# Seven half-size products in place of eight in block A's x^T phi(k), with its operand sums on VectorE

## The chip, the cores and the metric

The kernel runs on one core of a Trainium2 chip. Its time is the device time of one launch in microseconds; the kernel before takes 199.45 us (median of three runs, 199.34 to 199.52).

## The reference

Two blocks of linear attention, A and B, share the input x (2048 x 640) and have weights of their own; a gate computed from x mixes their outputs. There are 32 heads of 20 columns. Products take bfloat16 operands.

```python
qkv = (x @ wqkv)                                   # q, k, v, each 2048 x 640
phi = lambda t: jnp.where(t > 0, t + 1, jnp.exp(t)) + 1e-6
pq, pk = phi(q), phi(k)
kv  = jnp.einsum("bhsd,bhse->bhde", pk, v)         # per head 20 x 20
z   = jnp.einsum("bhsd->bhd", pk)
num = jnp.einsum("bhqd,bhde->bhqe", pq, kv)
den = jnp.einsum("bhqd,bhd->bhq", pq, z)[..., None] + 1e-6
block = (num / den) @ wo
g = sigmoid((x * gate_w).sum(-1, keepdims=True))
out = g * a + (1 - g) * b                          # a, b: the two blocks
```

## The kernel before

v is never formed. Since v = x wv, the sum over the rows of phi(k)^T v is taken as wv^T (x^T phi(k)): the kernel computes G = x^T phi(k), a 640 x 640 matrix whose inner dimension is the 2048 rows, then `kvt_pass` multiplies it with wv and masks it to the heads (KVT), and `m_unit` multiplies KVT with wo into M. The output is a product of the normalised phi(q) with M for both blocks, itself computed from quarter blocks with operand sums (class `Pair`, L431 to L477).

On the chip the 2048 rows are 16 chunks of 128 (ST), the 640 columns are five blocks of 128 (DT) or two halves of 320 (HF). `xn` holds x with rows on the partitions, `xT` its transpose, `pk` holds phi(k) by rows, `pqT` holds phi(q) transposed, `GT` holds G by row blocks of 128.

PSUM is used as four slots of two banks (`ps`, L63). A slot is handed out in turn or by number, and a new use waits until the last reader of the old one is done.

The stages of block A, in the order in which TensorE runs them:

- `k_chunk` (L195), 16 times: ten matmuls of 320 columns into a slot, then `phi` (L179): ScalarE takes exp out of PSUM into e; VectorE takes min(e, 1) + 1e-6 in place (L183), and then max(t + 1 + 1e-6, e), reading t out of PSUM (L184). Blocks of q for the first half of the rows (`q_block`, `q_unit`) are mixed in among them.
- `q_pass` (L492): five `q_unit`s for the second half of the rows (ten matmuls of 512 columns, `phi` on 128 x 1024); between them the gate's logits (`gate_pass`), the column sums of phi(k) (`z_rows`, zA) and their selection by head (`z_pass`, zsA).
- `g_all` (L506): five row blocks of G by `g_pass` (L246), each 16 chunks times two halves, 32 matmuls of 320 columns into one slot, evacuated by ScalarE. After the first block `rec_pass` (L338) makes the denominators (denA, 40 matmuls), which VectorE multiplies with the gate's factor and inverts (rT). Then come five `norm_unit`s (L387), two in each of the third and fourth blocks and one ahead of the fifth: eight small matmuls (exA) spread the inverses over two slots; VectorE multiplies phi(q) with the first slot directly out of PSUM, and with the second out of a bfloat16 copy (ex) that ScalarE makes.
- `p_diff` (L360): two passes of VectorE for the output's operands (D3).
- Block B's `k_chunk`s begin; `kvt_pass(0)` stands after the second of them in the program, and the `m_unit`s of A stand further on among the rest.

Block B follows with the same passes, and the output pairs close the kernel.

Up to the output stage the order on each engine is chosen by a scheduler at build time, from its own costs; only the output stage stands in a `manual_schedule`, where instructions keep the order of the program. Each engine runs its instructions in the order that it was given. Weights of the next stage are loaded by SP when the tile of the stage before has been read for the last time (wqB after q_pass).

Of the kernel before, what the change touches and what calls it, by code (L numbers as in the profile page):

```python
# [8 lines left out]
P = 128  # L9
FP32 = mybir.dt.float32  # L10
BF16 = mybir.dt.bfloat16
ACT = mybir.ActivationFunctionType
ALU = mybir.AluOpType

S, D, H = 2048, 640, 32
Dh = D // H
DT = D // P
ST = S // P
NB = 4
CB = 4  # L20
HB = 512
HF = D // 2
JW = 120
NJ = 6
EPS = 1e-6
RB = 256
SH = S // 2
# [3 lines left out]
def kernel(  # L31
# [11 lines left out]
    nc = tc.nc  # L43
# [4 lines left out]
    persist = ctx.enter_context(tc.tile_pool(name="persist", bufs=1))  # L48
    wpool = ctx.enter_context(tc.tile_pool(name="wpool", bufs=1))
    work = ctx.enter_context(tc.tile_pool(name="work", bufs=2))  # L50
# [12 lines left out]
    def ps(name, slot=None):  # L63

        return ps_raw(name, slot).bitcast(FP32).rearrange("p (b n) -> p b n", b=2)

    xT = persist.tile([P, DT, S], BF16, name="xT")
    xn = persist.tile([P, ST, D], BF16, name="xn")
    pk = persist.tile([P, ST, D], BF16, name="pk")
    pqT = [persist.tile([P, DT, S], BF16, name=f"pqT{b}") for b in "AB"]  # L70
    GT = persist.tile([P, DT, D], BF16, name="GT")
    KVT = persist.tile([P, NJ, D], BF16, name="KVT")
    M = [persist.tile([P, DT, D], BF16, name=f"M{b}") for b in "AB"]
# [6 lines left out]
    gwr = persist.tile([P, DT, H], BF16, name="gwr")  # L80
    zero = persist.tile([P, HB], BF16, name="zero")
    grow = persist.tile([1, D], BF16, name="grow")
    D3 = persist.tile([P, DT, S // 2], BF16, name="D3")
    TM = [None] * 4
    ge = [persist.tile([P, 2 * RB], FP32, name=f"ge{b}") for b in "AB"]

# [4 lines left out]
    nc.vector.memset(zero[:], 0.0)  # L91
    nc.vector.memset(ones[:], 1.0)
    nc.vector.memset(KVT[:], 0.0)
    xb0 = x2[0:CB * P, :].rearrange("(p q) d -> p q d", q=CB)
    wk = [None, None]
    wv = [None, None]
    wq = [None, None]
# [15 lines left out]
    for n in range(1, NB):  # L113
        for c in range(DT):
            nc.sync.dma_start_transpose(
                out=xT[:, c, n * HB:(n + 1) * HB], in_=x2[n * HB:(n + 1) * HB, c * P:(c + 1) * P]
# [8 lines left out]
    for sign, base in ((1, 0), (-1, Dh - 1)):  # L125
        nc.gpsimd.affine_select(
            out=maskE[:], in_=maskE[:], pattern=[[sign * P, DT], [-sign * Dh, H]],
# [3 lines left out]
    for r in range(4):  # L131
        rows = slice(32 * r, 32 * r + 32)
        for sign, base in ((1, 0), (-1, Dh - 1)):
            nc.gpsimd.affine_select(
                out=E4[rows], in_=E4[rows], pattern=[[sign, D]],
# [8 lines left out]
    def gate_columns():  # L144

        gps = ps("gps")
        for c in range(DT):
            nc.tensor.matmul(  # L148
                gps[:, 0, c * H:(c + 1) * H], lhsT=grow[0:1, c * P:(c + 1) * P], rhs=ones[0:1, :], start=True, stop=True
            )  # L150
        nc.vector.tensor_copy(out=gwr[:], in_=gps[:, 0, 0:DT * H].rearrange("p (c h) -> p c h", h=H))
# [24 lines left out]
        copy = nc.scalar.copy if eng == "act" else nc.vector.tensor_copy  # L176
        copy(out=xT[:, :, i * P:(i + 1) * P], in_=pt[:, 0:D].rearrange("p (c n) -> p c n", c=DT))

    def phi(dst, src, n):  # L179

        e = work.tile([P, 2, n], BF16, tag="e", name="e", bufs=3)
        nc.scalar.activation(out=e[:], in_=src, func=ACT.Exp)  # L182
        nc.vector.tensor_scalar(e[:], e[:], 1.0, EPS, op0=ALU.min, op1=ALU.add)  # L183
        nc.vector.scalar_tensor_tensor(out=dst, in0=src, scalar=1.0 + EPS, in1=e[:], op0=ALU.add, op1=ALU.max)  # L184

    def k_mm(b, i, c, pt, hf):
# [8 lines left out]
    def k_chunk(b, i):  # L195
        pt = ps(f"k{'AB'[b]}")
        for hf in range(2):
            for c in range(DT):
                k_mm(b, i, c, pt, hf)
        k_done(b, i, pt)  # L200
# [14 lines left out]
        for i in range(2):  # L215
            k_done(0, i, pts[i])

    def q_unit(b, m, h):

        pt = ps(f"q{'AB'[b]}")  # L220
        for u in range(2):
            for c in range(DT):
                n = 2 * h + u
                nc.tensor.matmul(  # L224
                    pt[:, u, :], lhsT=wq[b][:, c, m * P:(m + 1) * P], rhs=xT[:, c, n * HB:(n + 1) * HB],
                    start=(c == 0), stop=(c == DT - 1),
                )
        phi(pqT[b][:, m, h * 2 * HB:(h + 1) * 2 * HB].rearrange("p (b n) -> p b n", b=2), pt, HB)

    def q_block(b, m, n):  # L230

# [14 lines left out]
    def g_pass(b, c, slot, between=None):  # L246

        pt = ps(f"g{'AB'[b]}", slot)
        for i in range(ST):
            if between is not None and i == ST // 2:  # L250
                between()
            for hf in range(2):
                g_mm(c, i, hf, pt)
        evac(GT[:, c, :], pt, "act")

    def g_mm(c, i, hf, pt):
        nc.tensor.matmul(  # L257
            pt[:, hf, 0:HF], lhsT=xn[:, i, c * P:(c + 1) * P], rhs=pk[:, i, hf * HF:(hf + 1) * HF],
            start=(i == 0), stop=(i == ST - 1),
        )  # L260

    def g_last(b, c, slots):

# [74 lines left out]
    def rec_pass(b, zsel, slot):  # L338

        pt = ps(f"den{'AB'[b]}", slot)  # L340
        for h in range(2):
            by_group(pt[:, 0, h * RB:(h + 1) * RB], zsel, pqT[b], h)
        rts = []
        for h in range(2):
            part = slice(h * RB, (h + 1) * RB)
            d1 = work.tile([P, RB], FP32, tag="d1", name="d1")
            nc.vector.scalar_tensor_tensor(
                out=d1[:], in0=pt[:, 0, part], scalar=EPS, in1=ge[b][:, part], op0=ALU.add, op1=ALU.mult
            )
            rT = work.tile([P, RB], BF16, tag="rT", name="rT")  # L350
            with nc.allow_low_precision(reason="a fp32 reciprocal, stored as the bf16 that multiplies bf16"):
                nc.vector.reciprocal(out=rT[:], in_=d1[:])
            rts.append(rT)
        return rts

    def add_rows(dst, a, b, op):
        nc.vector.tensor_tensor(out=dst, in0=a, in1=b, op=op)

    def p_diff():

        for rows in (slice(0, HB), slice(HB, SH)):
            up = slice(SH + rows.start, SH + rows.stop)
            add_rows(D3[:, :, rows], pqT[0][:, :, rows], pqT[0][:, :, up], ALU.subtract)

# [24 lines left out]
    def norm_unit(b, parts, rts, slots):  # L389

        pts = [ps(f"ex{'AB'[b]}", s) for s in slots]
        for k, (m, h) in enumerate(parts):
            for j in range(4):
                nc.tensor.matmul(  # L394
                    pts[j // 2][:, j % 2, k * RB:(k + 1) * RB], lhsT=E4[32 * j:32 * j + 32, m * P:(m + 1) * P],
                    rhs=rts[h][32 * j:32 * j + 32, :], start=True, stop=True,
                )
        (m0, h0), (m1, h1) = parts
        for jj in range(2):
            src = pts[jj][:].rearrange("p j (k n) -> p j k n", n=RB)  # L400
            if h0 == h1:
                r0 = h0 * 2 * HB + jj * HB
                dst = pqT[b][:, m0:m1 + 1, r0:r0 + HB].rearrange("p k (j n) -> p j k n", n=RB)
            else:
                dst = pqT[b][:, m0, :].rearrange("p (k u j n) -> p u j k n", k=2, u=2, n=RB)[:, jj]
            if jj == 1:
                ex = work.tile([P, 2, 2, RB], BF16, tag="ex", name="ex")
                nc.scalar.copy(out=ex[:], in_=src)
                src = ex[:]
            nc.vector.tensor_tensor(out=dst, in0=src, in1=dst, op=ALU.mult)  # L410
# [68 lines left out]
    def load_w(b, which, eng):  # L479
        lo = {"q": 0, "k": D, "v": 2 * D}[which]  # L480
        t = wpool.tile([P, DT, D], BF16, tag="w" + which, name=f"w{which}{'AB'[b]}")
        eng.dma_start(out=t[:], in_=wq_dram[b][:, :, lo:lo + D])
        return t
# [8 lines left out]
    def q_pass(b, units):  # L492

        units = list(units)
        q_unit(b, *units.pop(0))
        if b == 0:
            gate_pass()
        zr = z_rows(b)
        for k in range(2):
            q_unit(b, *units.pop(0))  # L500
        zsel = z_pass(b, zr)
        for m, h in units:
            q_unit(b, m, h)
        return zsel

    def g_all(b, zsel):  # L506

        units = [((m, h), (m + 1, h)) for h in range(2) for m in (0, 2)] + [((DT - 1, 0), (DT - 1, 1))]

        def norm():  # L510
            norm_unit(b, units.pop(0), rts, (2, 3))

        g_pass(b, 0, 1)
        rts = rec_pass(b, zsel, 2)
        g_pass(b, 1, 0)
        for c in range(2, DT):
            norm()
            if b == 1 and c == DT - 1:
                g_last(b, c, (1, 0))
            else:  # L520
                g_pass(b, c, (c + 1) % 2, norm if c < DT - 1 else None)
        assert not units
# [7 lines left out]
        for m in (0, 2):  # L530
            q_block(0, m, n)
    q_unit(0, DT - 1, 0)
    for i in range(ST // 2, ST):
        if i == ST - 1:
            gate_columns()
        k_chunk(0, i)
    for n in range(1, NB):
        nc.sync.dma_start(
            out=xn[:, n * CB:(n + 1) * CB, :], in_=x2[n * HB:(n + 1) * HB, :].rearrange("(q p) d -> p q d", p=P)
        )  # L540
    wv[0] = load_w(0, "v", nc.sync)
    load_wo(0, nc.sync)
    wk[1] = load_w(1, "k", nc.sync)
    zsel = q_pass(0, [(m, 1) for m in range(DT)])
    wq[1] = load_w(1, "q", nc.sync)
    g_all(0, zsel)
    p_diff()


# [11 lines left out]
    zsel = q_pass(1, [(m, h) for h in range(2) for m in range(DT)])  # L561
    for tag, ks in (("wk", (0, 3)), ("wq", (1, 2))):
        t = wpool.tile([P, 2, DT, HF], BF16, tag=tag, name="TM" + tag)
# [12 lines left out]
    with tc.manual_schedule():  # L576
# [35 lines left out]
        for i in range(1, half):  # L612
            p, after = pairs[i], pairs[i + 1] if i + 1 < half else None
# [45 lines left out]
```

## Time and profile before

| | us |
|---|---|
| median of 3 runs | 199.45 (199.34 to 199.52) |
| the profiled execution | 200.06 |
| its span, first to last instruction | 198.3 |
| x^T phi(k) of A, from its first matmul to block B's first, by the chain of waits | 53.12 to 78.35 |
| granted TensorE clock | 1.0 of full speed throughout |

In the tables of the profile PE is TensorE's matmuls, PEld its weight loads, DVE is VectorE, ACT ScalarE, POOL GpSimd and SP the engine that issues most transfers. A line of a group gives the source line, engine and operation, what it writes and reads, shapes and types, how often, then the busy time in us and the mean of one in ns, then the idle time just before and what ended it. A window line gives, after its length, the busy time and the number of instructions of PE, PEld, DVE, ACT and POOL, then the granted clock, the share of the transfer engines' time and GB/s. A line of the list of waits gives who waited for whom, the total, how often and the longest. The chain of waits is followed back from the last instruction, at each step to what released it.

### The profile page before, as it was taken

Reading aid. Unit: us, or ns where it says so; the run is one execution under the profiler, and the core shown is the slowest. Engines: PE = TensorE matmul, PEld = TensorE weight load, DVE = VectorE, ACT = ScalarE, POOL = GpSimd, SP = SyncE. Lnnn points to the kernel's source line nnn. Section 1 sums busy time; section 2 is a strip of 40 time slices with the busy share of each in tenths; the row PEclk is TensorE's granted clock in tenths of the full one; section 3 lists DMA queues with packets and bytes.
Section 4 is the critical chain, followed back from the end, with each engine's and each line's share of the span. In section 5 each row is a group of like instructions: output and inputs, shape, how many; then the busy total and the mean of one; then the engine's idle time right before and its main releaser. Section 6 shows DMA issues by size and latency. Waiting matters only on the chain.

```text
span 198.3 us, 3641 instructions
## 1 busy us (share of the span) xinstructions
PE 192.0 (97%) x1518; PEld 123.2 (62%) x1525; DVE 140.4 (71%) x223; ACT 75.1 (38%) x103; POOL 9.2 (5%) x23
## 2 busy tenths in 40 slices
PE   7899999999999999999999999999999999999992
PEld 3556557654576667777774444576667777777771
DVE  4287869866748778667678777748779797885453
ACT  2245455453412443366553445413443421112210
POOL 7920000000000000000000000000000000000000
PEclk9999999999999999999999999999999999999999
DMA  6968479950040000140053000000000002212221
GB/s 194 292 139 105 94 197 373 223 167 3 8 159 3 0 0 3 12 153 3 0 117 75 0 0 0 2 3 0 3 0 0 3 0 90 78 69 82 80 70 66
DMA packets 18189, 14.21 MB, mean 72 GB/s; under 512 B 8782, under 2 KB 18046, under 8 KB 18174
## 3 DMA queue, kind: packets, MB, share of 16 engines
q1 hardware_dynamic: 17566, 13.17, 25.4%
q10 hardware_dynamic: 576, 0.82, 1.2%
q8 instruction: 12, 0.20, 0.4%
q14 instruction: 3, 0.02, 0.0%
q0 software_dynamic: 32, 0.00, 0.0%
HBM read 9.40 MB, written 2.62 MB: 61 GB/s over the span
## 4 chain that ended last, share of the span: by engine, by line
PE 94%; DMA 3%; SPq 0%; issue 0%; DVE 0%
PE gB L257 11%; PE gA L257 11%; PE kB L187 11%; PE qB L224 11%; PE kA L187 11%; PE qA L224 7%; PE oz L421 5%; PE ox L421 5%; PE oy L421 5%; PE qA L235 4%; PE ow L421 3%; DMA wkA<-in_A_wqkv_dram 3%; PE mA L333 1%; PE exA L394 1%; PE exB L394 1%; PE mid L333 1%
## 5 line engine op out<-in xcount | busy, mean ns | idle before, releaser
L187 PEld LDWEIGHTS <-xT 128*128 128x128 bf16 x320 | 30.9, 98 | 14.0 <-issue 0.9
L257 PEld LDWEIGHTS <-xn 128*128 128x128 bf16 x320 | 30.3, 98 | 14.1 <-issue 2.5
L183 DVE TENSOR_SCALAR e<-e 128x640 bf16<-128x640 bf16 (+1 forms) x52 | 19.3, 370 | 18.6 <-ACT e L182 17.5
L187 PE MATMUL kA<-wkA,xT 128*128 128x320 bf16 x160 | 23.0, 299 | 1.1 <-DMA wkA<-in_A_wqkv_dram 0.8
L257 PE MATMUL gB<-pk,xn 128*128 128x320 bf16 x160 | 22.9, 299 | 0.0
L257 PE MATMUL gA<-pk,xn 128*128 128x320 bf16 x160 | 22.9, 299 | 0.0
L187 PE MATMUL kB<-wkB,xT 128*128 128x320 bf16 x160 | 22.9, 299 | 0.0
L224 PE MATMUL qB<-xT,wqB 128*128 128x512 bf16 x97 | 21.9, 379 | 0.2
L224 PEld LDWEIGHTS <-wqB 128*128 128x128 bf16 x100 | 9.6, 98 | 11.4 <-issue 0.3
L182 ACT ACTIVATE e<-kA 128x640 bf16<-128x640 f32 x16 | 11.3, 705 | 13.4 <-PE kA L187 13.4
L182 ACT ACTIVATE e<-kB 128x640 bf16<-128x640 f32 x16 | 11.3, 704 | 11.7 <-PE kB L187 11.7
L182 ACT ACTIVATE e<-qA 128x1024 bf16<-128x1024 f32 x10 | 10.2, 1024 | 13.5 <-PE qA L224 8.4
L182 ACT ACTIVATE e<-qB 128x1024 bf16<-128x1024 f32 x10 | 10.2, 1024 | 13.1 <-PE qB L224 10.7
L184 DVE SCALAR_TENSOR_TENSOR pk<-kA,e 128x640 bf16<-128x640 f32 x16 | 13.2, 825 | 1.9 <-PE gps L148 0.5
L184 DVE SCALAR_TENSOR_TENSOR pk<-kB,e 128x640 bf16<-128x640 f32 x16 | 13.2, 824 | 1.6
L224 PE MATMUL qA<-xT,wqA 128*128 128x512 bf16 x58 | 13.5, 379 | 0.1
L184 DVE SCALAR_TENSOR_TENSOR pqTB<-qB,e 128x1024 bf16<-128x1024 f32 x10 | 12.3, 1225 | 1.0
L184 DVE SCALAR_TENSOR_TENSOR pqTA<-qA,e 128x1024 bf16<-128x1024 f32 x10 | 12.2, 1225 | 1.0
L455 ACT COPY u<-ox 128x320 f32<-128x320 f32 x8 | 3.4, 426 | 20.9 <-PE ox L421 20.9
L224 PEld LDWEIGHTS <-wqA 128*128 128x128 bf16 x60 | 5.7, 98 | 6.7 <-issue 0.3
L421 PEld LDWEIGHTS <-pqTB 128*128 128x128 bf16 x80 | 7.8, 98 | 3.0
L421 PEld LDWEIGHTS <-xT 128*128 128x128 bf16 x80 | 7.8, 98 | 3.0
(97 smaller groups left out, 226.6 us busy)
## 6 DMA issues: line engine op xcount, KB each, us to landing
out_dram<-osb SPq DMA_DIRECT2D x15, 160.0 KB, 1.8
xn<-in_A_x_dram SPq DMA_DIRECT2D x3, 640.0 KB, 5.9
wqA<-in_A_wqkv_dram SPq DMA_DIRECT2D x1, 800.0 KB, 6.6
wvA<-in_A_wqkv_dram SPq DMA_DIRECT2D x1, 800.0 KB, 9.4
wkB<-in_B_wqkv_dram SPq DMA_DIRECT2D x1, 800.0 KB, 4.5
wqB<-in_B_wqkv_dram SPq DMA_DIRECT2D x1, 800.0 KB, 4.7
wvB<-in_B_wqkv_dram SPq DMA_DIRECT2D x1, 800.0 KB, 4.7
woA<-in_A_wo_dram SPq DMA_DIRECT2D x1, 750.0 KB, 11.9
```

The costliest lines, as they stand in the source:

```text
L182: nc.scalar.activation(out=e[:], in_=src, func=ACT.Exp)
L183: nc.vector.tensor_scalar(e[:], e[:], 1.0, EPS, op0=ALU.min, op1=ALU.add)
L184: nc.vector.scalar_tensor_tensor(out=dst, in0=src, scalar=1.0 + EPS, in1=e[:], op0=ALU.add, op1=ALU.max)
L187: nc.tensor.matmul(pt[:, hf, 0:HF], lhsT=xT[:, c, i * P:(i + 1) * P], rhs=wk[b][:, c, hf * HF:(hf + 1) * HF], start=(c == 0), stop=(c == D ...
L224: nc.tensor.matmul(pt[:, u, :], lhsT=wq[b][:, c, m * P:(m + 1) * P], rhs=xT[:, c, n * HB:(n + 1) * HB], start=(c == 0), stop=(c == DT - 1),)
L235: nc.tensor.matmul(pt[:, u, :], lhsT=wq[b][:, c, (m + u) * P:(m + u + 1) * P], rhs=xT[:, c, n * HB:(n + 1) * HB], start=(c == 0), stop=(c ...
L257: nc.tensor.matmul(pt[:, hf, 0:HF], lhsT=xn[:, i, c * P:(c + 1) * P], rhs=pk[:, i, hf * HF:(hf + 1) * HF], start=(i == 0), stop=(i == ST - 1),
L333: nc.tensor.matmul(dst, lhsT=KVT[:rows, j, c * P:(c + 1) * P], rhs=wo_sb[b][:rows, j, hf * HF:(hf + 1) * HF], start=(k == 0), stop=(k == 1),)
L394: nc.tensor.matmul(pts[j // 2][:, j % 2, k * RB:(k + 1) * RB], lhsT=E4[32 * j:32 * j + 32, m * P:(m + 1) * P], rhs=rts[h][32 * j:32 * j + ...
L421: nc.tensor.matmul(dst, lhsT=left[:, c, r0:r0 + P], rhs=right[:, c, :], start=(first and c == 0), stop=(c == DT - 1), skip_group_check=not ...
L455: nc.scalar.copy(out=self.u2[:], in_=self.at("x"))
```

## The change

Of the five row blocks of A's G, the last (c = 4) keeps its 32 matmuls and is now computed first. The other four form a 512 x 640 matrix that is cut in quarters: rows in two groups of two blocks, columns in two halves of 320, and the inner dimension, the 16 row chunks, in two halves of eight. Seven products of quarters (Strassen's scheme in Winograd's form) replace the eight, each of 16 matmuls of 320 columns. Their operands are four sums of quarters of x (`x_sum`, SX) and four of phi(k) (`k_sum`, TK), in bfloat16 on VectorE. SX lies in the tiles of D3 and M, TK in the tile of block B's phi(q), all of which are written later. Three of the seven products write on into a slot that still holds an earlier one, after that one was read.

What is evacuated changes too: ScalarE copies the first product (p1) and, later, that slot again into G; five quarter sums are VectorE adds of a slot and a float32 tile (u2, u3 and three quarters of G).

In four of the five `q_unit`s of A's `q_pass`, `phi` is `lifted`: ScalarE computes t + 1 + 1e-6 as a second pass over PSUM (Identity with a bias), and VectorE's last step is a max of two bfloat16 tiles. In A's norm units ScalarE now copies both slots, not one.

From `gate_columns` to the end of `g_all(0, ...)` the program stands in a `manual_schedule`, so the engines follow its order there.

```diff
-    def phi(dst, src, n):
+    def phi(dst, src, n, lifted=False):
         e = work.tile([P, 2, n], BF16, tag="e", name="e", bufs=3)
         nc.scalar.activation(out=e[:], in_=src, func=ACT.Exp)
+        if lifted:
+            nc.scalar.activation(out=dst, in_=src, func=ACT.Identity, bias=lift[:])
         nc.vector.tensor_scalar(e[:], e[:], 1.0, EPS, op0=ALU.min, op1=ALU.add)
+        if lifted:
+            nc.vector.tensor_tensor(out=dst, in0=dst, in1=e[:], op=ALU.max)
+            return
         nc.vector.scalar_tensor_tensor(out=dst, in0=src, scalar=1.0 + EPS, in1=e[:], op0=ALU.add, op1=ALU.max)
...
+    def x_sum(k):
+        x11, x21 = [xn[:, 0:hc, n:n + ic] for n in (0, ic)]
+        x12, x22 = [xn[:, hc:ST, n:n + ic] for n in (0, ic)]
+        a, b, op = {
+            1: (x21, x22, ALU.add), 2: (SX[1], x11, ALU.subtract),
+            3: (x11, x21, ALU.subtract), 4: (x12, SX[2], ALU.subtract),
+        }[k]
+        add_rows(SX[k], a, b, op)
+    def k_sum(k):
+        b11, b12 = [pk[:, 0:hc, n * HF:(n + 1) * HF] for n in range(2)]
+        b21, b22 = [pk[:, hc:ST, n * HF:(n + 1) * HF] for n in range(2)]
+        a, b = {1: (b12, b11), 2: (b22, TK[1]), 3: (b22, b12), 4: (b21, TK[2])}[k]
+        add_rows(TK[k], a, b, ALU.subtract)
+    def g_prod(pt, left, right, first):
+        for i in range(hc):
+            for n in range(2):
+                nc.tensor.matmul(
+                    pt[:, n, 0:HF], lhsT=left[:, i, n * P:(n + 1) * P], rhs=right[:, i, :],
+                    start=(first and i == 0), stop=(i == hc - 1), skip_group_check=not first,
+                )
+    def g_strassen(norm):
...
+        def add(dst, pt, sb):
+            nc.vector.tensor_tensor(out=dst, in0=pt[:, :, 0:HF], in1=sb[:], op=ALU.add)
+        even, odd = ps("gs0", 0), ps("gs1", 1)
+        g_prod(even, x11, b11, True)
+        p1 = temp("p1")
+        nc.scalar.copy(out=p1[:], in_=even[:, :, 0:HF])
+        g_prod(odd, SX[2], TK[2], True)
+        u2 = temp("u2")
+        add(u2[:], odd, p1)
+        k_sum(4)
+        norm()
+        g_prod(even, x12, b21, False)
+        nc.scalar.copy(out=GT[:, 0:2, lo], in_=even[:, :, 0:HF])
+        norm()
+        x_sum(4)
+        g_prod(odd, SX[3], TK[3], False)
+        u3 = temp("u3")
+        add(u3[:], odd, p1)
+        norm()
+        even = ps("gs0", 0)
+        g_prod(even, SX[1], TK[1], True)
+        add(GT[:, 2:4, hi], even, u3)
+        norm()
+        g_prod(odd, x22, TK[4], False)
+        add(GT[:, 2:4, lo], odd, p1)
+        g_prod(even, SX[4], b22, False)
+        add(GT[:, 0:2, hi], even, u2)
+        norm()
...
-            if jj == 1:
+            if jj == 1 or b == 0:
                 ex = work.tile([P, 2, 2, RB], BF16, tag="ex", name="ex")
                 nc.scalar.copy(out=ex[:], in_=src)
...
         for k in range(2):
-            q_unit(b, *units.pop(0))
+            if b == 0:
+                x_sum(1 + k)
+            q_unit(b, *units.pop(0), b == 0)
         zsel = z_pass(b, zr)
-        for m, h in units:
-            q_unit(b, m, h)
+        for k, (m, h) in enumerate(units):
+            if b == 0 and k < 2:
+                (k_sum, x_sum)[k](2 + k)
+            q_unit(b, m, h, b == 0)
...
+        if b == 0:
+            g_pass(b, DT - 1, 1)
+            k_sum(3)
+            rts = rec_pass(b, zsel, 2)
+            g_strassen(norm)
+            assert not units
+            return
...
-    for i in range(ST // 2, ST):
-        if i == ST - 1:
-            gate_columns()
+    for i in range(hc, ST - 1):
         k_chunk(0, i)
...
-    zsel = q_pass(0, [(m, 1) for m in range(DT)])
-    wq[1] = load_w(1, "q", nc.sync)
-    g_all(0, zsel)
+    with tc.manual_schedule():
+        gate_columns()
+        k_chunk(0, ST - 1)
+        k_sum(1)
+        zsel = q_pass(0, [(m, 1) for m in range(DT)])
+        wq[1] = load_w(1, "q", nc.sync)
+        g_all(0, zsel)
     p_diff()
```

More of the change, by code (lines that the diff above doesn't have):

```diff
@@ L82 @@
     grow = persist.tile([1, D], BF16, name="grow")
-    D3 = persist.tile([P, DT, S // 2], BF16, name="D3")
+    D3 = persist.tile([P, DT, SH], BF16, name="D3")
+    d3_flat = D3[:].rearrange("p c s -> p (c s)")
+    m_flat = [t[:].rearrange("p c d -> p (c d)") for t in M]
+    hc, ic = ST // 2, 2 * P
+    SX = {k: t[:, o:o + hc * ic].rearrange("p (i c) -> p i c", i=hc)
+          for k, t, o in ((1, d3_flat, 0), (2, d3_flat, hc * ic), (3, m_flat[0], 0), (4, m_flat[1], 0))}
+    t_flat = pqT[1][:].rearrange("p c s -> p (c s)")
+    TK = {k: t_flat[:, n * hc * HF:(n + 1) * hc * HF].rearrange("p (i d) -> p i d", i=hc)
+          for n, k in enumerate((1, 2, 3, 4))}
+    lift = persist.tile([P, 1], FP32, name="lift")
     TM = [None] * 4
@@ L93 @@
     nc.vector.memset(KVT[:], 0.0)
+    nc.vector.memset(lift[:], 1.0 + EPS)
     xb0 = x2[0:CB * P, :].rearrange("(p q) d -> p q d", q=CB)
@@ L216, in k_first, with q_unit @@
             k_done(0, i, pts[i])
-    def q_unit(b, m, h):
+    def q_unit(b, m, h, lifted=False):
         pt = ps(f"q{'AB'[b]}")
@@ L227, in q_unit @@
                 )
-        phi(pqT[b][:, m, h * 2 * HB:(h + 1) * 2 * HB].rearrange("p (b n) -> p b n", b=2), pt, HB)
+        phi(pqT[b][:, m, h * 2 * HB:(h + 1) * 2 * HB].rearrange("p (b n) -> p b n", b=2), pt, HB, lifted)
     def q_block(b, m, n):
@@ L260, in g_mm, with temp @@
         )
+    def x_sum(k):
[19 more added lines that the diff above has]
+    def g_strassen(norm):
+        x11, x12 = [xn[:, k:k + hc, 0:ic] for k in (0, hc)]
+        x22 = xn[:, hc:ST, ic:2 * ic]
+        b11 = pk[:, 0:hc, 0:HF]
+        b21, b22 = [pk[:, hc:ST, n * HF:(n + 1) * HF] for n in range(2)]
+        lo, hi = slice(0, HF), slice(HF, D)
+        def temp(name):
+            return work.tile([P, 2, HF], FP32, tag="gt", name=name, bufs=3)
+        def add(dst, pt, sb):
[26 more added lines that the diff above has]
+        norm()
     def g_last(b, c, slots):
```

## The prediction

> **What bounds the kernel now.** I read the page first: busy times and the chain that ended last.
>
> ```profile
> PE 192.0 (97%) x1518; PEld 123.2 (62%) x1525; DVE 140.4 (71%) x223; ACT 75.1 (38%) x103; POOL 9.2 (5%) x23
> PE 94%; DMA 3%; SPq 0%; issue 0%; DVE 0%
> ```
>
> TensorE is on the chain 94% of the time, VectorE almost never. So a matmul taken out should shorten the span, unless it uncovers a wait. The chain in order of time over the changed stage (start, duration, what):
>
> ```profile
> 53.12 4.35 PE gA L257 x32
> 57.47 1.21 PE denA L158 x40
> 58.67 4.45 PE gA L257 x32
> 63.13 0.33 PE exA L394 x8
> 63.46 2.28 PE gA L257 x16
> ...
> 73.90 4.45 PE gA L257 x32
> 78.35 2.72 PE kB L187 x20
> ```
>
> No gap: 20 matmuls of 320 columns take 2.72, that is 0.136 each. Next, how full VectorE (third of the busy times) is beside it, in three windows, and its only long waits there, from the list of waits for 38 to 90 us:
>
> ```profile
> 42.00:53.00 11.00, 10.95 (x117) 5.82 (x115) 7.43 (x12) 5.18 (x6) 0.00 (x0) 1.00 0.18 64
> 53.00:58.60 5.60, 5.60 (x73) 3.97 (x71) 2.47 (x3) 1.72 (x2) 0.00 (x0) 1.00 0.48 146
> 58.60:78.00 19.40, 19.40 (x171) 12.61 (x168) 15.49 (x16) 6.84 (x8) 0.00 (x0) 1.00 0.01 2
> DVE e L183 <- ACT e L182: 6.7, 8, 1.7
> DVE pqTA L410 <- PE exA L394: 3.5, 5, 0.8
> DVE d L347 <- PE denA L158: 2.8, 1, 2.8
> ```
>
> VectorE works 25.4 of these 36 us; about 10 are free. The rows, shapes kept apart, that price the new work (busy, mean ns):
>
> ```profile
> L184 DVE SCALAR_TENSOR_TENSOR pqTA<-qA,e 128x1024 bf16<-128x1024 f32 x10 | 12.2, 1225 | 1.0
> L184 DVE SCALAR_TENSOR_TENSOR pk<-kA,e 128x640 bf16<-128x640 f32 x16 | 13.2, 825 | 1.9 <-PE gps L148 0.5
> L410 DVE TENSOR_TENSOR pqTA<-ex,pqTA 128x1024 bf16<-128x1024 bf16 x5 | 3.4, 688 | 0.3
> L357 DVE TENSOR_TENSOR D<-pqTA 128x2560 bf16<-128x2560 bf16 x2 | 2.9, 1484 | 0.0
> L357 DVE TENSOR_TENSOR TMwk<-MA 128x1600 bf16<-128x1600 bf16 x1 | 1.0, 981 | 0.0
> L281 DVE TENSOR_TENSOR zr<-zA,E 128x640 bf16<-128x640 f32 x1 | 0.8, 818 | 0.0
> L182 ACT ACTIVATE e<-qA 128x1024 bf16<-128x1024 f32 x10 | 10.2, 1024 | 13.5 <-PE qA L224 8.4
> L244 ACT CAST GT<-gA 128x640 bf16<-128x640 f32 x5 | 3.5, 692 | 13.9 <-PE gA L257 13.9
> ```
>
> **TensorE.** Four row blocks of 32 matmuls (128) become seven products of 16 (112). 16 x 0.136 = **2.18 us removed**. The five exA groups stay (0.33 each), and so does everything else on TensorE.
>
> A rule speaks against this step. The Trainium skill, "Perfetto Trace Analysis", Identifying the Most-Contended Engine, says matmul busy time is a poor measure of nearness to the limit and that the share of weight loading is a better one. By it the 62% above would leave room, and in the extreme the gain here would be nothing, 199.45. The chain without a gap is the nearer evidence, and I go by it.
>
> **VectorE.** Added: four sums over phi(k) quarters (128x2560), 4 x 1.485 = 5.94. The row of 1600 has the same runs of 320, and lies on the same line as the row of 2560. Four sums over x quarters (128x2048): between these rows, 0.981 + 448 x (1.484 - 0.981)/960 = 1.22, so 4.88; their runs of 256 have no row of their own. Upper bound for both: one element at a time as the PSUM rows go, (1225 - 825)/384 = 1.04 ns each, 2.29 and 2.82. Lower bound: as taken, since no row of two-tensor work is faster. Five adds of a PSUM bank pair and a float32 tile at 0.82 (zr): 4.10; upper bound 1.0, the measured 0.49 for 320 columns twice. Taken away: four of q's last steps fall from 1.225 to a two-tensor max in bf16, and five norm multiplications from 1.225 to 0.69: 9 x 0.535 = 4.8. Net **10.1 us more**.
>
> A max of two tensors has no row; nearest is the multiplication of the same shape, 0.69, upper bound the 1.225 it replaces. I take 0.69. The Trainium skill, "VectorE: DVE Perf Modes", What auto-detection actually checks, has the pace follow from operand type and step and not from the operation; by it the sum is the one below, and no trace here shows it.
>
> **ScalarE.** Added: four Identity passes over q (1.02 each, from the exp of the same shape; upper bound 1.225, VectorE's), five norm copies (1.02), two copies of a bank pair (0.69). Gone: four evacuations (0.69). Net +7.8 on an engine with 13.7 busy in the 36 us.
>
> The lift memset (one column) lies in VectorE's idle 1.25 us ahead of the first xT copy. SP and POOL issue the same transfers in the same order; wqB waits for the last reader of wqA as before. The x rows that the sums read are in SBUF: their transfers are issued by 26.7 and land in a median 5.9, and the first x sum stands at 46.
>
> **Laying it out.** Net totals don't say what waits, so I placed the instructions of each engine in the order of the changed program. Rules from the timeline of before: a VectorE instruction starts 0.07 before its predecessor's end (12.55 + 0.82, next 13.29), ScalarE's 0.1 before; both start 0.05 after TensorE's end in the chain (57.47, copy at 57.51); TensorE resumes 0.14 after VectorE (pk done 41.83, lg at 41.97). Start times:
>
> ```
> VectorE: K1 41.7, zr 45.5, X1 46.3, max 48.3, X2 49.0, max 50.6, K2 51.5, max 53.4, X3 54.0, max 55.6, K3 56.3,
>   d 58.7, rT 59.2, d 60.9, rT 61.3 (ends 63.05), u2 63.2, K4 63.9, norm1 65.4 66.0, norm2 67.5 68.4, X4 69.0,
>   u3 70.2, norm3 70.9 71.5, add 72.1, norm4 72.9 73.7, add 74.3, last add 75.8, norm5 77.1, D3 77.8, norm5 79.2, D3 80.1
> TensorE: g 53.12, den 57.47, P1 58.67, P2 60.95, ex1 63.13, 63.46, ex2 65.74, 66.07, ex3 68.35, 68.68, ex4 70.96, 71.29, 73.57, ex5 75.75
> ```
>
> - Up to the denominators VectorE is packed, but K3 ends at 57.75 and d could not start before 58.72 anyway: margin 1.0.
> - u2 must be read before the product at 66.07 writes on into its bank: done 64.0. u3 before 71.29: done 70.97, plus 0.14: margin 0.2. An exA group needs both ScalarE copies of the one before; ex3's second half is the tightest, copy done 68.32, needed 68.52.
> - ex5 ends at 76.08. Before, the kB chunks begin at 78.35: a gain of 2.27 here (2.18 and a few hundredths of rounding).
>
> **What comes back.** In the changed program TensorE's order after ex5 is one kB matmul, 12 kvA matmuls, two kB chunks, the other kvA. kvA uses the bank pair and the GT columns of the last add, 75.80 + 0.82 = 76.62, plus 0.14. TensorE is there at 76.22: **0.54 wait**. Before, 20 kB matmuls covered the last evacuation. Queued behind it are the kB chunks; behind those the whole rest. Next, VectorE owes norm5 and two D3 passes (1.485 each, at 75.85 to 78.7 before). The fourth kB chunk needs the bank of the first, whose last phi step waits behind the second D3: done 82.33, TensorE ready at 82.17, **0.30**. The sixth needs that of the third, behind the KVT masks: **0.14**. Then VectorE catches up (two chunks: 2 x 1.17 of VectorE in 3.27 of TensorE). Sum: -2.18 + 0.98 = **-1.2**. The profiled execution took 200.06 (span 198.3, 1.76 around it), 0.61 above the median of 199.45; the difference is taken off the median: **198.3**.
>
> **Rivals.**
> 1. None of the three waits bites (the add overlaps more than laid out, TensorE's first kB matmuls last longer): 199.45 - 2.18 = 197.3. For it: each wait is under 0.6, near what my start rules can resolve; against it, the kvA wait follows from data alone.
> 2. The max runs at 1.225: four times 0.535 later. The denominators then wait 0.14 and ex3 0.41: -1.2 + 0.55, 198.8.
> 3. Slower: VectorE becomes the bound because the x sums, gathered in runs of 256, go one element at a time (2.29). The first three then start the denominators late (0.75 of wait), the fourth holds u3 and thereby the sixth product (0.94), ex3 0.41: 2.1 more, 200.3; with the phi(k) sums at 2.82 too, 7.4 more, 205.7. It decides from about 2.05 us per x sum, where the added waits reach 1.2. For it: VectorE has some 33 us of work in the 34 to 76. Against: D3 and TM sums, also strided, keep the double pace.
> 4. Gain and waits cancel, 199.4: the same three waits each about 0.4 longer. For it: three engines now hand over with margins of 0.2 to 1.0.
>
> **Numbers.** Forecast 0.67; rival 1 0.10, rival 2 0.06, rival 3 0.11, rival 4 0.06. The forecast alone spans 197.7 to 198.9: 0.5 of waits less, 0.6 more. The range goes down to rival 1 and up past 2 and 4: 197.3 to 199.7. About 0.2% (0.4 us) can be told from no change: faster (under 199.05) has rivals 1 and 2 and the forecast but for 0.01, 0.82; same has that 0.01 and 0.05 of rival 4, 0.06; slower has rival 3 and the last 0.01 of rival 4, 0.12.
>
> **What would show it.** Right: 112 gs matmuls beside 32 of gA, ex5 about 2.2 earlier than at present, one TensorE wait of about half a microsecond on the last GT add, x sums near 1.22, phi(k) sums near 1.485, max near 0.69. Wrong: x sums near 2.3, TensorE waiting on rT or at the sixth product, kB chunks waiting on pk through several rounds, or matmuls of the seven products farther apart than 0.136.

## The result and the profile after

| | before | changed |
|---|---|---|
| median, 13 runs each | 199.59 (199.34 to 200.25) | 198.80 (198.44 to 199.28) |
| ratio | | 0.9961 [0.9949, 0.9973], that is -0.78 us [-0.54, -1.02] |
| the profiled execution | 200.06 | 199.17 |
| its span | 198.3 | 197.2 |
| start of the first gate matmul to the start of the last output add, in the trace | 156.69 | 155.59 |

Faster, as forecast, and inside the range; the gain is 0.8 us where 1.2 was forecast. The last row of the table is the stretch that I compare from here on, called the body: the point at which the gate's matmuls start lies between 37.5 and 39.0 us in the profiles of this case (but for one kernel, told below), and where the chain runs over the transfer of the first weights (wkA) it moves with it (landed at 6.79 and start at 37.97 in the changed kernel, at 7.99 and 38.97 in the run with the written order below). That noise is not the change's. The body is 1.10 shorter, and it repeats: second profiles of the two kernels give 156.69 and 155.60.

From the page of the changed kernel, the busy times and the shares of the chain that ended last:

```profile
PE 190.8 (97%) x1502; PEld 121.9 (62%) x1509; DVE 148.6 (75%) x237; ACT 82.5 (42%) x110; POOL 9.2 (5%) x23
PE 91%; DMA 3%; DVE 2%; issue 1%; ACT 1%; SPq 0%
```

There are 16 matmuls fewer, and VectorE and ScalarE have come onto the chain with a few per cent. Where, the chain over the changed stage shows (start, duration, what):

```profile
53.03 4.35 PE gA L272 x32
57.38 1.21 PE denA L168 x40
58.58 4.45 PE gs L298 x32
63.04 0.33 PE exA L476 x8
63.37 2.28 PE gs L298 x16
...
68.26 0.39 PE exA L476 x8
...
71.26 4.45 PE gs L298 x32
75.71 0.39 PE exA L476 x8
76.10 1.00 ACT ex L490
77.12 0.70 DVE pqTA L492
77.85 1.49 DVE D L439
...
81.50 0.83 DVE pk L199
82.37 2.88 PE kB L202 x20
```

How long the stage takes is best read from the timeline, between the starts of two matmuls: from the first behind the denominators to the first of block B's kB. Before:

```profile
58.61 4.52 PE L257 MATMUL gA<-pk,xn 128*128 128x320 bf16 x32
78.19 2.88 PE L187 MATMUL kB<-wkB,xT 128*128 128x320 bf16 x20
```

Changed:

```profile
58.52 2.35 PE L298 MATMUL gs<-pk,xn 128*128 128x320 bf16 x16
75.98 0.31 PE L202 MATMUL kB<-wkB,xT 128*128 128x320 bf16 x1
```

That is 19.58 and 17.46, so the stage itself gave 2.12. It is the 2.18 of 16 matmuls less 0.06: the third exA group (0.39 in the chain, where the others take 0.33) waits for the second of ScalarE's copies of the group before it. (The 0.39 of the fifth is no such wait; it counts up to the start of the copy behind it.) Four of the seven products, the third, fourth, sixth and seventh, and not three as the section on the change has it, write on into a slot that holds an earlier one; none of them waited, the gs matmuls stand 0.136 apart throughout.

Behind the stage the chain leaves TensorE: the fourth chunk of phi(k) of block B waits for a bank, and the bank for VectorE's second D pass (of `p_diff`). The timeline, by engine, gives the two larger waits in brackets, with what ended them:

```profile
75.75 0.83 DVE L315 TENSOR_TENSOR GT<-gs,u 128x640 bf16<-128x640 f32 x1 [0.88 <-PE gs L298]
76.63 0.79 PE L389 MATMUL kvA<-GT,wvA 128*128 128x120 bf16 x12 [0.34 <-DVE GT L315]
82.37 0.84 PE L202 MATMUL kB<-wkB,xT 128*128 128x320 bf16 x5 [0.20 <-DVE pk L199]
```

The brackets count from the modelled end of the last matmul, so they are smaller than what is lost. Adding up the matmuls queued ahead instead, TensorE could have begun kvA at 76.12 and began at 76.63, which is 0.51; the fourth chunk 82.00 and 82.37, 0.37; the sixth 85.63 and 85.78, 0.15. Together: -2.12 + 0.51 + 0.37 + 0.15 = -1.09, against -1.10 measured for the body.

VectorE's room, in the same three windows as before (its busy time is the third):

```profile
42.00:53.00 11.00, 10.95 (x117) 5.79 (x111) 10.03 (x14) 8.11 (x9) 0.00 (x0) 1.00 0.17 63
53.00:58.60 5.60, 5.60 (x74) 4.00 (x72) 4.72 (x7) 2.72 (x3) 0.00 (x0) 1.00 0.49 146
58.60:78.00 19.40, 19.06 (x171) 12.41 (x172) 16.52 (x21) 10.92 (x12) 0.00 (x0) 1.00 0.01 2
```

31.3 of 36 us, where it had 25.4. And what the new work costs (mean of one in ns after the bar):

```profile
L194 ACT ACTIVATE pqTA<-qA,lift 128x1024 bf16<-128x1024 f32 x4 | 4.4, 1108 | 0.0
L197 DVE TENSOR_TENSOR pqTA<-pqTA,e 128x1024 bf16<-128x1024 bf16 x4 | 2.8, 692 | 0.9 <-ACT pqTA L194 0.6
L439 DVE TENSOR_TENSOR D<-xn 128x2048 bf16<-128x2048 bf16 x1 | 1.2, 1214 | 0.0
L439 DVE TENSOR_TENSOR pqTB<-pk 128x2560 bf16<-128x2560 bf16 x2 | 3.0, 1482 | 0.0
L315 DVE TENSOR_TENSOR u<-gs,p 128x640 f32<-128x640 f32 x2 | 1.6, 820 | 0.2 <-PE gs L298 0.2
```

So the body explains a gain of 1.1. Most of the 0.3 between that and the medians lies outside the span, and is taken up after the experiments.

### The profile page after: what moved, and what is told of

It is laid out like the page before. It is cut to its first block, busy times and chain, and to the rows that moved or that the text cites. A ratio compares the mean times of both kernels' runs of the same rounds, so it can differ in the third digit from the quotient of the medians.

```text
span 197.2 us, 3638 instructions
## 1 busy us (share of the span) xinstructions
PE 190.8 (97%) x1502; PEld 121.9 (62%) x1509; DVE 148.6 (75%) x237; ACT 82.5 (42%) x110; POOL 9.2 (5%) x23
## 4 chain that ended last, share of the span: by engine, by line
PE 91%; DMA 3%; DVE 2%; issue 1%; ACT 1%; SPq 0%
PE gB L272 11%; PE qB L239 11%; PE kA L202 11%; PE kB L202 9%; PE gs L298 8%; PE qA L239 7%; PE oz L503 6%; PE ox L503 6%; PE oy L503 6%; PE qA L250 4%; PE ow L503 3%; DMA wkA<-in_A_wqkv_dram 3%; PE gA L272 2%; PE mA L415 1%; PE exA L476 1%
## 5 line engine op out<-in xcount | busy, mean ns | idle before, releaser
L272 PEld LDWEIGHTS <-xn 128*128 128x128 bf16 x192 | 18.3, 98 | 8.4 <-issue 1.3
L490 ACT CAST ex<-exA 128x1024 bf16<-128x1024 f32 x10 | 9.6, 1017 | 5.8 <-PE exA L476 4.9
L503 PEld LDWEIGHTS <-pqTA 128*128 128x128 bf16 x80 | 7.7, 98 | 3.0
```

Source lines behind the costliest of these rows:

```text
L272: nc.tensor.matmul(pt[:, hf, 0:HF], lhsT=xn[:, i, c * P:(c + 1) * P], rhs=pk[:, i, hf * HF:(hf + 1) * HF], start=(i == 0), stop=(i == ST - 1),
L503: nc.tensor.matmul(dst, lhsT=left[:, c, r0:r0 + P], rhs=right[:, c, :], start=(first and c == 0), stop=(c == DT - 1), skip_group_check=not ...
```

## The experiments

My theory: TensorE sets the end of the stage, so each product is worth its matmuls; what comes back is three waits behind the stage, which come from the order on VectorE and TensorE there. Rivals: TensorE's time there is not the limit (the order alone, or VectorE, sets it); the waits are of the data and no order removes them. Ratios are against the kernel before, run beside each on the same chip; bodies are against 156.69 before and 155.59 changed.

**An eighth product.** The first product is computed twice into the same bank.

```diff
         g_prod(even, x11, b11, True)
+        g_prod(even, x11, b11, True)
         p1 = temp("p1")
```

> The changed kernel with its first product (P1, 16 matmuls) computed twice into the same banks, so that eight products run again; everything else, sums and order included, stays. Theory (TensorE sets the stage): 16 x 0.136 = 2.18 us more than the changed kernel's 198.8, so about 201.0, and the same 2.2 in the span; the three waits behind the stage stay as they are. Rival (VectorE's queue sets the stage, the matmul count is hidden): under 1 us more, 199 to 199.8. Rival (the gain comes from the order or from phi, not from the products): likewise well under 2.

Measured: 201.38 us, ratio 1.0056 [1.0036, 1.0075]; body 157.77, which is 2.18 above the changed kernel. The chain of this kernel, its first products:

```profile
58.54 6.62 PE gs L298 x48
65.16 0.33 PE exA L477 x8
```

16 matmuls more in the group, 2.17 longer (6.62 against 4.45), and everything behind is late by it. TensorE is the limit of the stage.

**All but the products.** The fixed order, the lifted phi and both norm copies stay; G is computed by its 160 matmuls, without operand sums.

```diff
-            if b == 0:
-                x_sum(1 + k)
...
-            if b == 0 and k < 2:
-                (k_sum, x_sum)[k](2 + k)
...
-            g_pass(b, DT - 1, 1)
-            k_sum(3)
-            rts = rec_pass(b, zsel, 2)
-            g_strassen(norm)
-            assert not units
-            return
+            pass
...
-        k_sum(1)
```

> Everything of the change but the products: fixed order, lifted phi, both norm slots copied by ScalarE, but A's G by the 160 matmuls of before and no operand sums. Theory: TensorE's stream is that of before and stays without gaps, so 199.6 as before, at most 0.2 more where two ScalarE copies and an evacuation stand ahead of an exA group. Rival (order, phi and norm bring the gain): 198.8 or near it.

Measured: 200.45, ratio 1.0001 [0.9977, 1.0025]; body 156.83, 0.14 over that of before; in its trace two of the five exA groups, the second and the fourth, wait 0.06 each, as the third does in the changed kernel. The other parts of the change give nothing by themselves; the gain is that of the products.

**The order behind the stage.** Block B's chunks, `kvt_pass(0)` and the M blocks in a written order, with the two D passes after chunks 6 and 8, and the chunks' slots turned by one so that the first one needs no bank of the last product.

```diff
-    def p_diff():
+    def p_diff(parts=(0, 1)):
...
-    p_diff()
-    turn[0] = 2
+    with tc.manual_schedule():
+        turn[0] = 1
         k_chunk(1, 0)
         k_chunk(1, 1)
         kvt_pass(0)
...
         for i in range(3, ST):
             k_chunk(1, i)
...
+            if i in (6, 8):
+                p_diff((i // 2 - 3,))
```

> The changed kernel, with what follows its last product put in a fixed order as well: block B's first two chunks use the slots that are free first (the third product slot, then the norm slots in the order in which they are copied), kvA comes after them, and the two D3 passes stand after chunks 6 and 8. Theory (the missing part of the 2.18 us is the wait for the last add, 0.51 in the trace, and the two waits behind D3, 0.37 and 0.15): all three go, 1.0 us less than the changed kernel, about 197.8, 1.8 below the kernel before. Rival (the part is lost elsewhere, in the start or in slower handovers): 198.6 to 198.8.

Measured: 198.93, ratio 0.9937 [0.9907, 0.9967]; body 155.04, only 0.55 better. The forecast missed. Up to B's q pass it had gained 0.91, most of the 1.03 of the three waits; then it lost 0.36 in one place. The chain of this kernel there, and two lines of its timeline:

```profile
118.84 5.20 PE qB L239 x24
...
124.06 1.03 ACT e L192
...
125.65 1.24 DVE pqTB L199
...
126.93 3.15 PE gB L272 x22
```

```profile
126.02 0.71 PE L272 MATMUL gB<-pk,xn 128*128 128x320 bf16 x4
126.93 4.51 PE L272 MATMUL gB<-pk,xn 128*128 128x320 bf16 x32 [0.20 <-DVE pqTB L199]
```

The chunks hand out slots in turn, so my shift by one also moved q's slots, and the slots of B's G by number did not move: the first row block of gB now took the slot that q's last unit but one had, and waited for its phi. Four gB matmuls run ahead of it; the last of them starts at 126.43 and the next at 126.93, 0.50 later in place of 0.136. That is the 0.36, and not the 0.75 that a later expectation states.

**Half of that order.** Only the first two chunks and `kvt_pass(0)` are written out, the D passes are left to the scheduler.

```diff
+    with tc.manual_schedule():
+        turn[0] = 1
+        k_chunk(1, 0)
+        k_chunk(1, 1)
+        kvt_pass(0)
     p_diff()
-    turn[0] = 2
-    k_chunk(1, 0)
-    k_chunk(1, 1)
-    kvt_pass(0)
```

> As the run with the fixed order behind the stage, but the D3 passes stay where the scheduler puts them, between and after the last norm steps. Laid out: the wait for the last add goes (0.51), but the fourth chunk's slot is now that of the first chunk, whose last phi step stands behind the second D3, and waits 0.85 in place of 0.37. Theory (the waits are one debt of VectorE, which only moves): within 0.2 of the changed kernel, 198.6 to 199.0. Rival (the waits are independent): 0.5 less, 198.3.

Measured: 199.82, ratio 0.9969 [0.9945, 0.9993]. From the first gA matmul to B's q pass 50.06, against 50.05 in the changed kernel: the wait on the last add is gone, and the wait of the fourth chunk behind the D passes has grown by as much, from 0.37 to 0.87. With the same loss of slots later the body is 155.97, worse by 0.38.

**The last order with the slots turned back.** As the third, and one line ahead of B's q pass:

```diff
+    turn[0] = (turn[0] + 1) % 4
     zsel = q_pass(1, [(m, h) for h in range(2) for m in range(DT)])
```

> The changed kernel with the fixed order behind the stage (as the earlier run with that order), and one slot skipped ahead of block B's q pass, so that its units use the slots that they had before. The earlier run gained 0.91 up to B's q pass and lost 0.75 of it there: B's first row block of G takes slot 1, and with the shifted turn that was the slot of q's last unit but one, whose phi ended at 126.9. Theory: with the turn restored that wait is gone and the 0.9 to 1.0 stays; from the gate's matmuls to the last add 154.6 us (155.59 in the changed kernel), about 197.9, 0.5% below the changed kernel run beside it. Rival (the wait at B's first row block follows from q's phi being late as a whole, not from the slot): 155.0, as the earlier run.

Measured: 198.24, ratio 0.9927 [0.9907, 0.9947]; body 154.69, 0.91 below the changed kernel. The changed kernel was run once more beside it.

> The changed kernel once more, beside the run with the restored slots, on the same chip and against the same runs of the kernel before. Theory: the start varies from execution to execution (the gate's matmuls began between 37.5 and 39.0 in the profiles so far) and the rest does not: 155.6 from there to the last add, and a ratio to the kernel before of 0.994 to 0.997.

Measured: 199.03, ratio 0.9964 [0.9947, 0.9981], body 155.60. The chain of the kernel with the slots turned back, from the fifth exA group on:

```profile
76.07 0.33 PE exA L476 x8
76.40 2.82 PE kB L202 x20
79.22 1.43 PE kvA L389 x30
80.66 4.08 PE kB L202 x30
```

None of the three waits is left: 20 kB matmuls cover the last add, as they covered the last evacuation before the change. The D passes lie where VectorE has time for them. Of the 2.18 of the products the body now has 2.00; the 0.06 at the third exA group stays, and a kB matmul at 96.38 comes 0.10 late. This version is faster than both, by its ratio 1.5 us under the kernel before.

**Each x sum twice**, to see whether VectorE becomes the bound at about the price of rival 3.

```diff
         add_rows(SX[k], a, b, op)
+        add_rows(SX[k], a, b, op)
```

> The changed kernel with each of the four x sums made twice (4 x 1.22 us more on VectorE, same result). Laid out as for the prediction, with 2.37 per sum: the first block waits 0.4 for zsel, the denominators 0.6 for the last max, ex3 0.4, the sixth product 1.0, in all 2.4 us more than the changed kernel, about 201.2, slower than the kernel before. Theory: VectorE's queue has about 1 us of margin in this stage, and past that it becomes the bound. Rival (VectorE is still far from the bound and its work hides): under 0.5 more, 199.3 at most.

Measured: 201.79, ratio 1.0092 [1.0074, 1.011]; body 158.14, 2.55 later. VectorE carries nearly the whole chain of this kernel from 42 to 74, here its end:

```profile
71.24 1.15 DVE MB L440
72.41 1.23 DVE MB L440
73.64 0.74 DVE u L316
...
74.42 4.51 PE gs L299 x32
```

The doubled fourth sum (MB) holds u3, and the sixth product waits for it: the mechanism of my slower rival, which had 2.1 for a sum of 2.29; a doubled one is 2.38 (1.15 + 1.23). TensorE waits in the four places of the expectation: 0.68 ahead of the first block, 0.63 in the denominators, 0.32 more than in the changed kernel at the third exA group and 0.92 ahead of the sixth product, 2.55 in all.

**phi of q as before** (`lifted` is not passed on):

```diff
-        phi(pqT[b][:, m, h * 2 * HB:(h + 1) * 2 * HB].rearrange("p (b n) -> p b n", b=2), pt, HB, lifted)
+        phi(pqT[b][:, m, h * 2 * HB:(h + 1) * 2 * HB].rearrange("p (b n) -> p b n", b=2), pt, HB)
```

> The changed kernel with q's phi as before in all units (no second pass on ScalarE; VectorE's last step out of PSUM, 1.225 in place of 0.69). Laid out: VectorE has 2.1 us more, K3 ends later and the denominators' division starts later, but only ex3 waits, 0.1. Theory: 0.1 to 0.4 more than the changed kernel, 198.9 to 199.2. Rival (VectorE has no margin at all): 2 us more, 200.9.

Measured: 199.15, ratio 0.9967 [0.995, 0.9984]; body 0.26 longer. The medians alone can't tell it from the changed kernel; the body falls in what was expected, and the 0.25 stand in the third exA group (0.64 from its start to the next product, in place of 0.39), where 0.1 was expected.

**The first slot of each norm unit out of PSUM by VectorE, as before.**

```diff
-            if jj == 1 or b == 0:
+            if jj == 1:
```

> The changed kernel with the first slot of each norm unit multiplied out of PSUM by VectorE as before (1.225 in place of 0.69, five times; five ScalarE copies fewer). Laid out: ex2 waits 1.0 for VectorE to free its slot, ex4 0.3, the first kB chunk 0.55, the fourth 0.3 less than now: 1.5 us more than the changed kernel, about 200.3, slower than the kernel before. Rival (VectorE's extra 2.7 us hide, or cost only at the end): under 0.6 more, 199.4 at most.

Measured: 199.84, ratio 0.9994 [0.9982, 1.0006]; body 156.64, 1.05 longer, where 1.5 was expected: the gain is gone. The second exA group waits 0.98 (1.0 expected), the fourth 0.11 (0.3), the first kB chunk 0.16 (0.55). VectorE is on the chain of this kernel, where TensorE was:

```profile
62.64 0.82 DVE u L315
63.47 1.40 DVE pqTB L439
64.87 3.47 DVE pqTA L492 x4
68.33 1.14 DVE MB L439
```

Behind these stand u3 and the norm multiplications that free the banks of exA. Without the copies on ScalarE, VectorE could not take the sums and leave a gain.

**No fixed order**: the same program, left to the scheduler.

```diff
-    with tc.manual_schedule():
+    if True:
```

> The changed kernel without its fixed order: the scheduler places the operand sums. It puts the first x sum among the first phi steps of the kA chunks, ahead of the fourth chunk's last step (13.7 us in the trace of before), although it reads rows of x whose transfer is issued at 25.5 us and takes about 6. Theory: VectorE stands at that sum until about 31, PSUM's four slots fill up within some 5 us, and TensorE loses about 12 to 14 us: about 211. Rival (the scheduler's order does as well as the fixed one): 198.8.

Measured: 220.66, ratio 1.1043 [1.1026, 1.106]. From the list of waits (who waited for whom: total, how often, longest) and from three windows (busy times as above, then the granted clock) of this kernel:

```profile
DVE MA L439 <- DMA xn<-in_A_x_dram: 19.6, 1, 19.6
PE qA L250 <- DVE pk L199: 19.1, 1, 19.1
```

```profile
24.70:31.30 6.60, 0.00 (x0) 0.00 (x0) 1.99 (x3) 0.00 (x0) 0.00 (x0) 0.50 0.87 274
31.33:36.40 5.07, 5.07 (x12) 1.73 (x12) 4.04 (x7) 1.31 (x2) 0.00 (x0) 0.50 1.06 306
40.00:50.00 10.00, 10.00 (x58) 5.47 (x56) 9.43 (x14) 4.56 (x6) 0.00 (x0) 1.00 0.00 0
```

The scheduler had put x sums into VectorE's early idle time. The one into MA reads the x rows, whose transfer SP issues only after its transposes at 24.7; VectorE stood from 9.67 to 29.31, the phi of k behind it, and TensorE 19.1 us behind that. When TensorE came back its granted clock was 0.50 for the first 5 us, and the first 20 q matmuls took 6.97 instead of 4.32. The sum of both, 19.1 + 2.65 = 21.8, is the difference of the median spans (218.6 against 196.8). I had expected 12 to 14: a sum that the scheduler put earlier than the one I looked at, and the clock. From the gate's matmuls on, which start at 59.65 here, this kernel has the body of the changed one, 155.60: the whole loss lies ahead, and in the stage itself the scheduler's order does as well. So what the fixed order does for this change is to keep the sums behind the arrival of the x rows. Alone it does nothing:

**The fixed order alone**, in the kernel before, and beside it the kernel before once more, as a measure of what a repeat gives.

```diff
-    for i in range(ST // 2, ST):
-        if i == ST - 1:
-            gate_columns()
+    for i in range(ST // 2, ST - 1):
         k_chunk(0, i)
...
-    zsel = q_pass(0, [(m, 1) for m in range(DT)])
-    wq[1] = load_w(1, "q", nc.sync)
-    g_all(0, zsel)
+    with tc.manual_schedule():
+        gate_columns()
+        k_chunk(0, ST - 1)
+        zsel = q_pass(0, [(m, 1) for m in range(DT)])
+        wq[1] = load_w(1, "q", nc.sync)
+        g_all(0, zsel)
```

> The kernel before with the fixed order alone, from the gate's columns to the end of A's G: TensorE's and ScalarE's order stay what they were, on VectorE two small instructions change places. Theory: the span stays (198.1 to 198.5 in the kernel before), ratio 1.000. If the additional 0.2 to 0.3 outside the span belongs to the fixed order, it shows here (1.9 or more); if it belongs to the new instructions or to the place in the measurement, this run has what the kernel before has when it is run in the same place.

> The kernel before itself, run in the place of an experiment. So far the time outside the span (device time less the span of the same execution) was 1.7 in the executions of the kernel before and 1.9 to 2.2 in the changed kernel and its variants. Theory (it belongs to the program): 1.7 here too, ratio 1.000. Rival (it belongs to the place in the measurement): 1.9 to 2.0, and a ratio of about 1.001.

Measured: 199.74, ratio 0.9999 [0.9987, 1.0011], and 199.71, ratio 1.0006 [0.9992, 1.002]. The body of both is 156.69, as before. These two were run for the time outside the span, the device time less the span of the same execution:

| | runs | median of device time less span |
|---|---|---|
| kernel before, beside the experiments | 11, 14, 17, 23 | 1.74, 1.72, 1.73, 1.74 |
| kernel before, as an experiment | 12 | 1.75 |
| fixed order alone | 12 | 1.75 |
| changed kernel | 13 and 12 | 2.00 and 1.93 |
| eighth product; all but the products | 6; 6 | 2.02; 1.93 |
| x sums twice; phi as before; norm as before | 4; 5; 10 | 1.88; 1.92; 1.90 |
| written order; half of it; slots turned back | 6; 6; 6 | 2.16; 2.17; 2.08 |
| no fixed order | 4 | 2.16 |

The changed program has 0.2 to 0.3 us more outside its span, in both sets of runs, and its variants 0.16 to 0.44 more. Neither the place of the run nor the fixed order makes it (it is there without that order too), nor the sums and products, since it is there without them. What all the programs that have it share is the column of constants and at least one of the lifted phi and the ScalarE norm copies (each of these two was taken out alone, and it stayed). I did not separate these; the cause is open.

## Why the prediction was right, and by how much it was off

- *TensorE, 2.18 removed.* Right: the stage is 2.12 shorter in the profiled run, and an added product costs 2.17 to 2.18. The rest is a margin that the layout had wrong. It gave the second half of the third exA group 0.2 to spare (copy done 68.32, needed 68.52); the copy was done at 68.21, but TensorE wanted it at the start of the group, 68.19, and waited until 68.26. From the first product to the first kB matmul 17.41 was laid out (58.67 to 76.08) and 17.46 measured. The rule weighed against this step (the Trainium skill, "Perfetto Trace Analysis", Identifying the Most-Contended Engine) judges by weight loading, and by the share of the peak's operations beside it, how near TensorE is to its peak. The 62% of weight loading did not tell here what a matmul taken out is worth; the chain over TensorE did.
- *VectorE's prices.* x sums 1.214 to 1.219 (forecast 1.22), phi(k) sums 1.479 to 1.483 (1.485), max 0.692 (0.69), adds 0.82 (0.82), all from neighbouring rows of the profile before. Durations added up, VectorE has 10.0 us more (10.1); the page's busy time grows by 8.2 only, since instructions that overlap by 0.07 are counted once. That the max has the pace of the multiplication of the same shape agrees with what the prediction cited (the Trainium skill, "VectorE: DVE Perf Modes", What auto-detection actually checks), 0.692 against 0.688.
- *ScalarE's price.* The Identity with a bias took 1.108, not 1.02. It cost nothing, as ScalarE is busy 21.8 of the 36 us. The nearest row was an exp without a bias tile.
- *The waits that come back.* All three came, where they were placed: 0.51 for 0.54, 0.37 for 0.30, 0.15 for 0.14. That they are a matter of order, and not of the data alone, the run with the slots turned back shows.
- *Rivals.* No waits: refuted by the two timeline rows. The max at 1.225 and the x sums at 2.29: refuted by their rows; the doubled x sums show that the mechanism is real. The measured 198.80 is also the number of rival 2, by chance: its cause, a max at 1.225, is not there. Gain and waits cancel: no, though taking the norm copies back does bring that about.
- *The step that was mis-sized.* "The difference is taken off the median." The body changed by -1.10, near the -1.2 of the sum; the medians by -0.78, since time outside the span grew by about 0.25. The prediction named the 1.76 around the span and took it as fixed; for this pair of programs it is not. The 198.80 is 0.5 above the 198.3. About 0.26 of it is this time outside the span, about 0.1 the body (the stage gave 0.06 less, the waits took 0.05 more), and 0.14 is that the kernel before has a median of 199.59 over 13 runs, where the forecast started from 199.45.

## What to carry to other kernels

Where the chain of waits lies on one engine without a gap, work taken off that engine counted nearly in full here (2.12 of 2.18); what comes back is found by asking which engine delivers the last operand at the seam behind the stage, and what stood there before as cover. Lay the other engines' instructions out one after another with prices from rows of the same type and step: sums of busy time would not have found the three waits, nor the place where doubling a sum bites. The seam is then worth an order of its own: cover for the last add and two passes moved were worth 0.91 here, nearly as much as the products had left, and a rotation of buffers shifted for it has to be turned back where buffers are taken by number.

## What was not expected of the hardware

- An Identity pass of ScalarE with a bias from a [128, 1] tile took 1108 ns on 128x1024, where the exp without one took 1024. The Trainium skill, "ScalarE: Activation LUTs", What ACT_TABLE_LOAD costs, states 93 ns for such an operand; the rows, which are of two functions, give 84.
- After 19.1 us without a matmul the granted clock was 0.50, and 20 matmuls of 512 columns took 6.97 us instead of 4.32. The Trainium skill, "TensorE: Matmul & The Clock Gate", What's actually happening, describes a half-rate state after idle time, which agrees with the 0.50.
- The time outside the span went with the program: 1.72 to 1.75 for the kernel before in every set of runs, 1.93 and 2.00 for the changed one. What makes it is open.
